# Decode attention on one core: K and V laid out as four heads of two batch rows, 16 partitions each

## The chip, the cores and the metric

The kernel runs on one core of a Trainium2 chip. The metric is the device time of one execution in microseconds (us). Several executions are timed and their median is given.

## The reference

One decode step for four batch rows (B = 4, one token each, width D = 640): layer norm, attention over a cache of Sk = 4096 keys with H = 32 heads of Dh = 128, a residual, layer norm, and a small MLP with the Mish activation. All inputs are bf16.

```
q = (layernorm(x) @ wq).reshape(B, 1, 32, 128).transpose(0, 2, 1, 3)
scores = einsum("bhqd,bhkd->bhqk", q, k_cache) * 128 ** -0.5
o = einsum("bhqk,bhkd->bhqd", softmax(scores), v_cache)
h = x + o.transpose(0, 2, 1, 3).reshape(B, 1, 4096) @ wo
a = layernorm(h) @ w1 + b1            # 640 -> 1728
out = h + (a * tanh(softplus(a))) @ w2
```

The K cache and the V cache hold 4 x 32 x 4096 x 128 values of 2 bytes each, 134.2 MB per cache. Every byte of both is read once.

## The kernel before, in words

The order of all instructions is written out by hand; each engine takes its own in that order.

**Tiling.** One group g is four heads (G = 4) of one batch row: hq, b = divmod(g, 4), 32 groups in all. A head's 4096 keys are spread over 32 partitions (PH = 32), 128 keys in each (R = 128), so K of a group is a tile of 128 partitions with 32 KB each, 4 MB, loaded by one DMA whose 128 rows lie one behind the other in the cache. V has the same layout. There are two K buffers and two V buffers (load_kv, L92 to L101). All these DMAs are issued from the queue of SyncE (SP), in program order: K of g + 2 when group g's products are done with their buffer, then V of g + 1. A DMA that has to wait for its buffer holds up those behind it on SP.

**Scores.** The queries come from q_chunk (L195) and q_broadcast (L209), once per four heads; they are spread to all partitions in qbs. In mul_and_sum VectorE multiplies K in place by the query (L367, two halves of the head dimension for each of two halves of the keys), and TensorE adds groups of columns with the identity matrix as weights, into PSUM (L374, eight matmuls for each product). finish_sum (L386) adds the last eight columns and leaves 128 scores per partition.

**Softmax.** softmax(g) takes the maximum per partition (L397), transposes it with a matmul (L399), takes the maximum per head (L404), spreads it to all partitions (L412, L414), and then ScalarE makes four exponentials per group, one for each head's 32 partitions (L417). Each writes its own column of e2[128 partitions, 128 keys, 4 heads], whose other columns are zero from the start, and its own column of the row sums rs2. Its two halves are put between the products of group g + 1.

**Probabilities times V.** pv_moving (L257) takes four keys per partition at a time: the weights are e2's 16 columns (4 keys x 4 heads), the moving operand is 512 columns of V. Four such matmuls use four disjoint ranges of rows of one PSUM bank p_ps (rows c0 to c0 + 15). pv_copy (L267) copies p_ps to SBUF, and add_blocks (L273) adds up the blocks that belong together with the matrix pick. row_sums (L296), normalise (L307), regroup (L332) and project (L348) follow once per four heads, the last with wo.

**End.** The last K group comes in two DMAs and the last V in four; half of the last V is worked on by pv_stationary (L284), with V as the weights. The weights of the MLP are loaded behind the last V (L502 to L507); w2r_sb is a rest of 64 rows. Then come the layer norm, the first MLP product (L563), the activation (up to L610), the second product (L625) and the output (L649).

Of the kernel before, what the change touches and what calls it, by code (L numbers as in the profile page):

```python
# [8 lines left out]
FP32 = mybir.dt.float32  # L9
# [7 lines left out]
def kernel(  # L17
# [23 lines left out]

    nc = tc.nc
# [4 lines left out]
    N = B * Sq  # L47
    DC = D // 128
    G = 4
    PH = 128 // G  # L50
    R = Sk // PH
    NP = 2
    RP = R // NP
    W = 512 // RP
    HQ = H // G
    NG = HQ * N
# [6 lines left out]
    VP = 4  # L63
    KBUFS = 2
    VBUFS = 2
# [17 lines left out]
    vpool = ctx.enter_context(tc.tile_pool(name="vpool", bufs=VBUFS))  # L83
# [8 lines left out]
    def load_kv(pool, tag, cache, g, parts):  # L92
        hq, b = divmod(g, N)
        t = pool.tile([128, R, Dh], BF16, tag=tag, name=f"{tag}{g}")
        view = cache[b, G * hq : G * (hq + 1)].rearrange("h (p r) d -> (h p) r d", p=PH)

        np_ = parts if g == NG - 1 else 1
        for i in range(np_):
            r0, r1 = i * R // np_, (i + 1) * R // np_
            nc.sync.dma_start(out=t[:, r0:r1, :], in_=view[:, r0:r1, :])  # L100
        return t  # L101

    def load_k(g):
        return load_kv(kpool, "kt", A_k_cache, g, NP)

    def load_v(g):
        return load_kv(vpool, "vt", A_v_cache, g, VP)
# [6 lines left out]
    kts, vts = {}, {}  # L114
    kts[0] = load_k(0)
    kts[1] = load_k(1)
    vts[0] = load_v(0)
# [14 lines left out]
    sel = consts.tile([N, N, G, 128], BF16)  # L132
    nc.vector.memset(sel[:, :, :, :], 0.0)
    e2 = [consts.tile([128, R, G], BF16, name=f"e2_{i}") for i in range(NE2)]
    for t in e2:
        nc.gpsimd.memset(t[:, :, :], 0.0)
    rs2 = consts.tile([128, NG, G], FP32)
    nc.gpsimd.memset(rs2[:, :, :], 0.0)
# [4 lines left out]
    for q in range(G):  # L143
        nc.vector.tensor_copy(
            out=sel[:, :, q, q * PH : (q + 1) * PH],
            in_=ident[0:N, 0:N].unsqueeze(2).to_broadcast([N, N, PH]),
        )
# [42 lines left out]
    q_all = consts.tile([N, H * Dh], BF16)  # L190

    def q_chunk(n):
        q_ps = ps.tile([N, QC], FP32, tag="qq")
        for c in range(DC):
            nc.tensor.matmul(  # L195
                q_ps[:, :],
                lhsT=xT[:, c, :],
                rhs=wq_sb[:, c, n * QC : (n + 1) * QC],
                start=(c == 0),
                stop=(c == DC - 1),  # L200
            )
        nc.scalar.copy(out=q_all[:, n * QC : (n + 1) * QC], in_=q_ps[:, :])  # L202

    def q_broadcast(hq):
        qb_ps = ps.tile([128, N * Dh], FP32, tag="qq")
        for b in range(N):
            for q in range(G):
                h = G * hq + q
                nc.tensor.matmul(  # L209
                    qb_ps[:, b * Dh : (b + 1) * Dh],  # L210
                    lhsT=sel[:, b, q, :],
                    rhs=q_all[:, h * Dh : (h + 1) * Dh],
                    start=(q == 0),
                    stop=(q == G - 1),
                )
        nc.scalar.copy(
            out=qbs[:, hq, :, :], in_=qb_ps[:, :].rearrange("p (b d) -> p b d", d=Dh)
        )

    qbs = consts.tile([128, HQ, N, Dh], BF16)  # L220
# [7 lines left out]
    for hq in Q_AT[-1]:  # L228
        q_chunk(hq)
        q_broadcast(hq)  # L230
# [7 lines left out]
    nc.vector.memset(p_ps[:, :], 0.0)  # L238
    pick = consts.tile([128, J * G], FP32)
    nc.vector.tensor_reduce(  # L240
        out=pick[:, :],
        in_=ident_f[:, :].rearrange("p (t i) -> p i t", t=T)[:, 0 : J * G, :],
# [5 lines left out]
    def ot_of(g):  # L248
        hq, b = divmod(g, N)
        if b == 0:  # L250
            ot[hq] = ps.tile([128, N, G], FP32, tag="ot", name=f"ot{hq}")
        return ot[hq][:, b, :]

    def pv_moving(g, r0, r1):
        for r in range(r0, r1, J):
            c0 = 128 // T * (r // J % T)
            nc.tensor.matmul(  # L257
                p_ps[c0 : c0 + J * G, :],
                lhsT=e2[g % NE2][:, r : r + J, :].rearrange("p j q -> p (j q)"),
                rhs=vts[g][:, r : r + J, :].rearrange("p j d -> p (j d)"),  # L260
                start=(r < J * T),
                stop=(r >= r1 - J * T),
            )

    def pv_copy(g):
        blocks[g] = work.tile([128, J * Dh], FP32, tag="p_sb", bufs=1, name=f"p_sb{g}")
        nc.scalar.copy(out=blocks[g][:, :], in_=p_ps[:, :])  # L267

    def add_blocks(g, stop=True):
        o = ot_of(g)  # L270
        p_sb = blocks.pop(g)
        for j in range(J):
            nc.tensor.matmul(  # L273
                o,
                lhsT=p_sb[:, j * Dh : (j + 1) * Dh],
                rhs=pick[:, j * G : (j + 1) * G],
                start=(j == 0),
                stop=(stop and j == J - 1),
            )
        return o  # L280

    def pv_stationary(g, o, r0):
        for r in range(r0, R):
            nc.tensor.matmul(  # L284
                o,
                lhsT=vts[g][:, r, :],
                rhs=e2[g % NE2][:, r, :],
                start=False,
                stop=(r == R - 1),
            )  # L290
# [3 lines left out]
    def row_sums(hq):  # L294
        l_ps = ps.tile([128, N, G], FP32, tag="small")
        nc.tensor.matmul(  # L296
            l_ps[:, :, :],
            lhsT=ones_f[:, :],
            rhs=rs2[:, hq * N : (hq + 1) * N, :],
            start=True,  # L300
            stop=True,
        )
        rls[hq] = work.tile([128, N, G], FP32, tag="rl", name=f"rl{hq}")
        nc.vector.reciprocal(out=rls[hq][:, :, :], in_=l_ps[:, :, :])  # L304
# [23 lines left out]
    def regroup(hq):  # L328
        o4_ps = ps.tile([128, G, N], FP32, tag="small", name=f"o4_{hq}")
        for q in range(G):  # L330
            for i in range(G):
                nc.tensor.matmul(  # L332
                    o4_ps[q * PH : (q + 1) * PH, i, :],
                    lhsT=ident4[:, i, :],
                    rhs=otn[:, hq, :, q],
                    start=True,
                    stop=True,
                )
# [19 lines left out]
    def mul_and_sum(g, part):  # L358

        hq, b = divmod(g, N)  # L360
# [4 lines left out]
        for k in range(NQ):  # L365
# [4 lines left out]
                in1=qbs[:, hq, b, d0 : d0 + DQ].unsqueeze(1).to_broadcast([128, RP, DQ]),  # L370
# [12 lines left out]
    def finish_sum(g, part):  # L383
        if part == 0:
            s_sbs[g] = work.tile([128, R], FP32, tag="s_sb", name=f"s_sb{g}")
        nc.vector.tensor_reduce(  # L386
            out=s_sbs[g][:, part * RP : (part + 1) * RP],
# [5 lines left out]
    def softmax(g):  # L393

        s_sb = s_sbs.pop(g)
        pm = work.tile([128, 1], FP32, tag="pm", name=f"pm{g}")
        nc.vector.tensor_reduce(out=pm[:, :], in_=s_sb[:, :], axis=AX.X, op=ALU.max)  # L397
        tr_ps = ps.tile([128, 128 + G], FP32, tag="tr", name=f"tr{g}")
# [3 lines left out]
        yield  # L402
        mx = work.tile([1, G], FP32, tag="mx", name=f"mx{g}")
        nc.vector.tensor_reduce(  # L404
            out=mx[:, :],
            in_=tr_ps[0:1, 0:128].rearrange("o (a b) -> o a b", a=G),
# [4 lines left out]
        nb_ps = tr_ps[:, 128 : 128 + G]  # L411
        nc.tensor.matmul(nb_ps, lhsT=nscale[:, :], rhs=mx[:, :], start=True, stop=True)  # L412
        nb = work.tile([128, G], FP32, tag="nbs", name=f"nbs{g}")
        nc.scalar.copy(out=nb[:, :], in_=nb_ps)  # L414
        for q in range(G):
            p0, p1 = q * PH, (q + 1) * PH
            nc.scalar.activation(  # L417
                out=e2[g % NE2][p0:p1, :, q],
                in_=s_sb[p0:p1, :],
                func=ACT.Exp,  # L420
                bias=nb[p0:p1, q : q + 1],
                scale=SCALE,
                accum_out=rs2[p0:p1, g, q : q + 1],
            )
        yield

    for g in range(NG):
        hq, b = divmod(g, N)
        for part in range(NP):
            now = mul_and_sum(g, part)  # L430
            before = None
            next(now)
            if part > 0:
                finish_sum(g, part - 1)
                if g >= 2:
                    add_blocks(g - 2)
                    if b == 1:
                        row_sums(hq - 1)
                        normalise(hq - 1)
                if g in PROJ_AT:  # L440
                    regroup(PROJ_AT[g])
            elif g >= 1:
                finish_sum(g - 1, NP - 1)
                before = softmax(g - 1)
                next(before)
            next(now)
            if before is not None:
                next(before)
# [3 lines left out]
        if 1 <= g < NG - 1:  # L452
            pv_moving(g - 1, 0, R)
            pv_copy(g - 1)
            vts.pop(g - 1)
        if g in PROJ_AT:
            project(PROJ_AT[g])
        if g + 1 < NG:
            vts[g + 1] = load_v(g + 1)
        for n in Q_AT.get(g, ()):  # L460
            q_chunk(n)
            q_broadcast(n)
# [28 lines left out]

    mlp = ctx.enter_context(tc.tile_pool(name="mlp", bufs=1))
# [18 lines left out]


    finish_sum(NG - 1, NP - 1)
    for _ in softmax(NG - 1):
        pass
    pv_moving(NG - 2, 0, R)
    pv_copy(NG - 2)
    row_sums(HQ - 1)
    add_blocks(NG - 2)

    R_LAST = R // 2
    pv_moving(NG - 1, 0, R_LAST)
    pv_copy(NG - 1)
    pv_stationary(NG - 1, add_blocks(NG - 1, stop=False), R_LAST)
# [156 lines left out]
```

## Time and profile before

| | |
|---|---|
| median of 3 runs | 668.12 us (667.93 to 669.77) |
| the profiled execution: its own time | 667.95 us |
| the profiled execution: its span, first to last instruction | 666.0 us |
| moved by DMA | 283.81 MB in 12871 packets, mean 426 GB/s |
| busy: PE (matmul) | 441.5 us, 66% |
| busy: PEld (weight load, beside PE) | 203.6 us, 31% |
| busy: DVE (VectorE) | 352.7 us, 53% |
| busy: ACT (ScalarE) | 114.9 us, 17% |
| mean granted TensorE clock | 0.847 |

How to read it. The span is cut into 40 slices; a digit is the busy share of a slice in tenths, 9 meaning 90% or more. The row DMA is the mean over the 16 DMA engines of the core, and GB/s is what they moved. A group line has the source line, the engine, the operation, output<-inputs by tile names, the shapes, the count, then the total busy time and the mean duration in ns, then the engine's idle time ahead of it and what ended most of that. The issue view lists DMAs by size with the median time from issue to landing. The chain of waits is followed back from the last instruction. Besides the instructions, the trace holds one record for each DMA packet: its start, duration and size.

### The profile page before, as it was taken

The page shows a single profiled execution, that of the slowest core. Times are in us where ns is not written, and L with a number is a line of the kernel's source. Part 1 is how long each engine was busy: PE and PEld are TensorE (multiplying, and loading weights), DVE is VectorE, ACT ScalarE, POOL GpSimd, SP SyncE. Part 2 cuts the span into 40 slices and gives each one's busy share as a digit, 9 for nine tenths or more (in the row PEclk, how much of TensorE's full clock was granted, in tenths as well). Part 3 has the DMA queues.
Part 4 walks back from the last instruction along what each step waited for, and adds up shares of the span by engine and source line. Part 5 has one row for each costly group of instructions (what it writes and reads, how often), then busy time and mean ns, then how long its engine had stood idle before and what let it go on. Part 6 is the DMA issues. An engine that isn't in the chain of part 4 may idle for free.

```text
span 666.0 us, 7149 instructions
## 1 busy us (share of the span) xinstructions
PE 441.5 (66%) x3105; PEld 203.6 (31%) x3105; DVE 352.7 (53%) x306; ACT 114.9 (17%) x352; POOL 2.4 (0%) x13
## 2 busy tenths in 40 slices
PE   0587777897566475377666857756557785667785
PEld 0233233343223232133322323322223332223345
DVE  2486454566645266246654545657444666455742
ACT  0022122122101111011111111111011111011141
POOL 1000000000000000000000000000000000000000
PEclk9998789798778877787777798778789797788985
DMA  9999999999999999999999999999999999999996
GB/s 376 441 434 421 434 440 433 420 436 439 436 419 436 425 434 432 429 437 426 437 433 432 427 435 440 423 432 437 438 424 431 436 438 427 430 433 438 425 418 263
DMA packets 12871, 283.81 MB, mean 426 GB/s; under 512 B 1379, under 2 KB 2087, under 8 KB 4008
## 3 DMA queue, kind: packets, MB, share of 16 engines
q1 hardware_dynamic: 12832, 283.36, 99.0%
q8 instruction: 24, 0.39, 0.2%
q14 instruction: 7, 0.06, 0.0%
q10 hardware_dynamic: 8, 0.01, 0.0%
HBM read 283.35 MB, written 0.01 MB: 425 GB/s over the span
## 4 chain that ended last, share of the span: by engine, by line
DMA 64%; PE 18%; DVE 17%; issue 1%; ACT 0%; SPq 0%; DVEq 0%
DMA kt<-in_A_k_cache_dram 59%; DVE kt L367 14%; PE s L374 14%; DMA w<-in_B_w_dram 3%; DMA vt<-in_A_v_cache_dram 3%; DVE s_sb L386 2%; PE tr L399 1%; PE p_ps L257 1%; PE ot L273 1%; DVE mx L404 0%; PE q_ps L195 0%; PE qb_ps L209 0%; DVE pm L397 0%; PE o L332 0%; ACT q_all L202 0%
## 5 line engine op out<-in xcount | busy, mean ns | idle before, releaser
L374 PE MATMUL s<-kt,ident 128*128 128x512 bf16 x1024 | 295.1, 440 | 193.9 <-DVE kt L367 191.5
L367 DVE TENSOR_TENSOR kt<-kt,qbs 128x4096 bf16<-128x4096 bf16 x128 | 291.5, 2279 | 238.0 <-DMA kt<-in_A_k_cache_dram 238.0
L374 PEld LDWEIGHTS <-ident 128*128 128x128 bf16 x1024 | 109.2, 110 | 337.5 <-issue 167.8
L417 ACT ACTIVATE e<-s_sb,nbs 32x128 bf16<-32x128 f32 x128 | 74.0, 578 | 2.5
L257 PE MATMUL p_ps<-vt,e 128*16 128x512 bf16 x1008 | 64.5, 401 | 0.0
L414 ACT COPY nbs<-tr 128x4 f32<-128x4 f32 x32 | 5.2, 162 | 326.9 <-PE tr L412 326.9
L386 DVE TENSOR_REDUCE s_sb<-s 128x64 f32<-128x512 f32 x64 | 43.5, 680 | 4.0 <-PE s L374 3.9
L267 ACT COPY p_sb<-p_ps 128x512 f32<-128x512 f32 x32 | 18.7, 585 | 154.7 <-PE p_ps L257 154.7
L273 PEld LDWEIGHTS ot<-pick,p_sb 128*128 128x128 f32 x256 | 33.8, 193 | 5.8 <-ACT p_sb L267 1.5
L257 PEld LDWEIGHTS <-e 128*16 128x16 bf16 x1008 | 23.2, 92 | 39.7 <-issue 20.2
L417 ACT ACTIVATION_READ_ACCUMULATOR e<-s_sb,nbs 32x1 f32 x128 | 32.2, 251 | 0.0
L273 PE MATMUL ot<-pick,p_sb 128*128 128x4 f32 x256 | 31.0, 244 | 0.9 <-ACT p_sb L267 0.7
L404 DVE TENSOR_REDUCE mx<-tr 1x4 f32<-1x128 f32 x32 | 8.9, 277 | 23.9 <-PE tr L399 23.9
L195 PE MATMUL q_ps<-wq_sb,xT 128*4 128x512 bf16 x40 | 11.0, 409 | 9.8 <-DMA wq_sb<-in_A_wq_dram 9.8
L399 PE MATMUL tr<-ident_f,pm 128*1 128x128 f32 x64 | 15.2, 329 | 1.2 <-DVE pm L397 1.2
L412 PEld LDWEIGHTS tr<-mx,nscale 1*128 1x128 f32 x64 | 9.4, 182 | 13.8 <-issue 11.4
L304 DVE RECIPROCAL rl<-l_ps 128x16 f32<-128x16 f32 x8 | 2.1, 257 | 21.0 <-PE l_ps L296 21.0
L209 PE MATMUL qb_ps<-q_all,sel 4*128 4x128 bf16 x128 | 9.2, 225 | 5.3 <-ACT q_all L202 5.3
L412 PE MATMUL tr<-mx,nscale 1*128 1x4 f32 x64 | 12.2, 258 | 0.4 <-DVE mx L404 0.4
L209 PEld LDWEIGHTS <-sel 4*128 4x128 bf16 x128 | 8.4, 98 | 9.1 <-issue 9.1
L202 ACT CAST q_all<-q_ps 4x512 bf16<-4x512 f32 x8 | 4.6, 574 | 34.5 <-PE q_ps L195 34.5
L399 PEld LDWEIGHTS tr<-ident_f,pm 128*1 128x1 f32 x64 | 2.8, 80 | 22.9 <-issue 22.9
(85 smaller groups left out, 77.6 us busy)
## 6 DMA issues: line engine op xcount, KB each, us to landing
kt<-in_A_k_cache_dram SPq DMA_DIRECT2D x31, 4096.0 KB, 25.1
vt<-in_A_v_cache_dram SPq DMA_DIRECT2D x31, 4096.0 KB, 33.1
wq_sb<-in_A_wq_dram SPq DMA_DIRECT2D x1, 5120.0 KB
wo_sb<-in_A_wo_dram SPq DMA_DIRECT2D x8, 640.0 KB, 33.9
kt<-in_A_k_cache_dram SPq DMA_DIRECT2D x2, 2048.0 KB
vt<-in_A_v_cache_dram SPq DMA_DIRECT2D x4, 1024.0 KB, 19.0
w<-in_B_w_dram SPq DMA_DIRECT2D x3, 640.0 KB, 17.8
w<-in_B_w_dram SPq DMA_DIRECT2D x1, 1296.0 KB, 25.8
```

Source lines behind the costliest of these rows:

```text
L195: nc.tensor.matmul(q_ps[:, :], lhsT=xT[:, c, :], rhs=wq_sb[:, c, n * QC : (n + 1) * QC], start=(c == 0), stop=(c == DC - 1),)
L209: nc.tensor.matmul(qb_ps[:, b * Dh : (b + 1) * Dh], lhsT=sel[:, b, q, :], rhs=q_all[:, h * Dh : (h + 1) * Dh], start=(q == 0), stop=(q == ...
L257: nc.tensor.matmul(p_ps[c0 : c0 + J * G, :], lhsT=e2[g % NE2][:, r : r + J, :].rearrange("p j q -> p (j q)"), rhs=vts[g][:, r : r + J, :]. ...
L267: nc.scalar.copy(out=blocks[g][:, :], in_=p_ps[:, :])
L273: nc.tensor.matmul(o, lhsT=p_sb[:, j * Dh : (j + 1) * Dh], rhs=pick[:, j * G : (j + 1) * G], start=(j == 0), stop=(stop and j == J - 1),)
L367: nc.vector.tensor_tensor(out=kt[:, :, d0 : d0 + DQ], in0=kt[:, :, d0 : d0 + DQ], in1=qbs[:, hq, b, d0 : d0 + DQ].unsqueeze(1).to_broadcas ...
L374: nc.tensor.matmul(s_ps[:, :, :], lhsT=ident[:, :], rhs=kt[:, :, d : d + W], start=(d == 0), stop=(d == Dh - W),)
L386: nc.vector.tensor_reduce(out=s_sbs[g][:, part * RP : (part + 1) * RP], in_=s_of.pop((g, part))[:, :, :], axis=AX.X, op=ALU.add,)
L399: nc.tensor.matmul(tr_ps[0:1, 0:128], lhsT=pm[:, :], rhs=ident_f[:, :], start=True, stop=True)
L404: nc.vector.tensor_reduce(out=mx[:, :], in_=tr_ps[0:1, 0:128].rearrange("o (a b) -> o a b", a=G), axis=AX.X, op=ALU.max,)
L412: nc.tensor.matmul(nb_ps, lhsT=nscale[:, :], rhs=mx[:, :], start=True, stop=True)
L417: nc.scalar.activation(out=e2[g % NE2][p0:p1, :, q], in_=s_sb[p0:p1, :], func=ACT.Exp, bias=nb[p0:p1, q : q + 1], scale=SCALE, accum_out=r ...
```

## The change

A unit is now four heads of two batch rows (NB = 2, P8 = 8 pairs of row and head), 16 units in all. Each pair has 16 partitions (PH = 16) with 256 keys each (R = 256). The two batch rows alternate by partition: partition 32 q + 2 x + b holds slice x of head q of batch row b. A K tile is half of a unit's keys, 32 KB per partition, with two buffers as before; V of a whole unit is 64 KB per partition in one buffer. As one access pattern can't describe both batch rows, every load is now two DMAs of 64 rows, one to the even and one to the odd partitions (t[b:128:NB]).

One exponential per unit covers all 128 partitions, and a product with a mask of ones and zeros spreads it over eight columns of e2. The row sums take the mask in the same way. The weights of pv_moving have 32 columns. The softmax of a unit stands behind its last sum, no longer between the next group's products, and V's matmuls follow it at once; then V of the next unit is loaded. V of the last two units is loaded in parts. The queries of four heads are kept in a small tile per chunk, and the broadcast for two batch rows takes half the matmuls.

```diff
-    PH = 128 // G
-    R = Sk // PH
+    NB = 2
+    P8 = NB * G
+    PH = 128 // P8
+    R = Sk // PH
+    KT = 2
+    RK = R // KT
...
-    def load_kv(pool, tag, cache, g, parts):
-        hq, b = divmod(g, N)
-        t = pool.tile([128, R, Dh], BF16, tag=tag, name=f"{tag}{g}")
-        view = cache[b, G * hq : G * (hq + 1)].rearrange("h (p r) d -> (h p) r d", p=PH)
-        np_ = parts if g == NG - 1 else 1
-        for i in range(np_):
-            r0, r1 = i * R // np_, (i + 1) * R // np_
-            nc.sync.dma_start(out=t[:, r0:r1, :], in_=view[:, r0:r1, :])
-        return t
+    def load_keys(t, cache, u, keys, dst):
+        hq, bp = divmod(u, N // NB)
+        k0, k1 = keys
+        for b in range(NB):
+            view = cache[NB * bp + b, G * hq : G * (hq + 1)].rearrange("h (p r) d -> (h p) r d", p=PH)
+            nc.sync.dma_start(out=t[b:128:NB, dst : dst + k1 - k0, :], in_=view[:, k0:k1, :])
+
+    def load_k(g):
+        u, k = divmod(g, KT)
+        t = kpool.tile([128, RK, Dh], BF16, tag="kt", name=f"kt{g}")
+        n = NP if g == NG - 1 else 1
+        for i in range(n):
+            r0, r1 = i * RK // n, (i + 1) * RK // n
+            load_keys(t, A_k_cache, u, (k * RK + r0, k * RK + r1), r0)
+        return t
+
+    v_sb = vpool.tile([128, R, Dh], BF16, name="v_sb")
+
+    def load_v(u, r0=0, r1=R):
+        load_keys(v_sb, A_v_cache, u, (r0, r1), r0)
...
+    mask = consts.tile([128, P8], BF16)
+        nc.vector.tensor_reduce(
+            out=mask[:, :].rearrange("p (b q) -> p b q", b=NB),
+            in_=ident[:, :].rearrange("p (q x b) -> p b q x", q=G, b=NB),
+            axis=AX.X,
+            op=ALU.add,
+        )
+    e1 = consts.tile([128, R], BF16)
+    e2 = [consts.tile([128, R, P8], BF16, name=f"e2_{i}") for i in range(NE2)]
...
-                p_ps[c0 : c0 + J * G, :],
-                lhsT=e2[g % NE2][:, r : r + J, :].rearrange("p j q -> p (j q)"),
-                rhs=vts[g][:, r : r + J, :].rearrange("p j d -> p (j d)"),
+                p_ps[c0 : c0 + J * P8, :],
+                lhsT=e2[u % NE2][:, r : r + J, :].rearrange("p j i -> p (j i)"),
+                rhs=v_sb[:, r : r + J, :].rearrange("p j d -> p (j d)"),
...
-        nc.scalar.copy(out=nb[:, :], in_=nb_ps)
-        for q in range(G):
-            p0, p1 = q * PH, (q + 1) * PH
-            nc.scalar.activation(
-                out=e2[g % NE2][p0:p1, :, q],
-                in_=s_sb[p0:p1, :],
-                func=ACT.Exp,
-                bias=nb[p0:p1, q : q + 1],
-                scale=SCALE,
-                accum_out=rs2[p0:p1, g, q : q + 1],
-            )
+        nb8 = work.tile([128, P8], FP32, tag="nb8", name=f"nb8_{u}")
+        nc.vector.tensor_tensor(out=nb8[:, :], in0=nb_ps, in1=mask[:, :], op=ALU.mult)
+        nb = work.tile([128, 1], FP32, tag="nbs", name=f"nbs{u}")
+        nc.vector.tensor_reduce(out=nb[:, :], in_=nb8[:, :], axis=AX.X, op=ALU.add)
+        nc.scalar.activation(
+            out=e1[:, :],
+            in_=s_sb[:, :],
+            func=ACT.Exp,
+            bias=nb[:, :],
+            scale=SCALE,
+            accum_out=rs[:, u : u + 1],
+        )
+        nc.vector.tensor_tensor(
+            out=e2[u % NE2][:, :, :],
+            in0=e1[:, :].unsqueeze(2).to_broadcast([128, R, P8]),
+            in1=mask[:, :].unsqueeze(1).to_broadcast([128, R, P8]),
+            op=ALU.mult,
+        )
...
         kts.pop(g)
         if g + 2 < NG:
             kts[g + 2] = load_k(g + 2)
-        if 1 <= g < NG - 1:
-            pv_moving(g - 1, 0, R)
-            pv_copy(g - 1)
-            vts.pop(g - 1)
+        if k == KT - 1:
+            finish_sum(g, NP - 1)
+            softmax(u)
         if g in PROJ_AT:
             project(PROJ_AT[g])
-        if g + 1 < NG:
-            vts[g + 1] = load_v(g + 1)
+        if k == KT - 1 and u < NU - 2:
+            pv_moving(u, 0, R, R)
+            pv_copy(u)
+            add_blocks(u)
+            if bp == N // NB - 1:
+                row_sums(hq)
+                normalise(hq)
+            if u + 1 < NU - 2:
+                load_v(u + 1)
+            else:
+                load_v(NU - 2, 0, RK)
+        elif k == KT - 1 and u == NU - 2:
+            load_v(u, RK, R)
+            pv_moving(u, 0, RK, R)
+            load_v(NU - 1, 0, RK)
...
+    u = NU - 1
+    pv_moving(u - 1, RK, R, R)
+    pv_copy(u - 1)
+    VQ = RK // 4
+    for r in range(RK, R, VQ):
+        load_v(u, r, r + VQ)
```

## The prediction

> **What bounds the kernel now.** I read the forty slices first, then the stretches, then the chain and the groups, then the DMA issues, and last the single packet records of the trace. The slices of the page:
>
> ```profile
> DMA  9999999999999999999999999999999999999996
> GB/s 376 441 434 421 434 440 433 420 436 439 436 419 436 425 434 432 429 437 426 437 433 432 427 435 440 423 432 437 438 424 431 436 438 427 430 433 438 425 418 263
> ...
> q1 hardware_dynamic: 12832, 283.36, 99.0%
> ```
>
> The 16 DMA engines are busy in every slice but the last. The stretches (from:to, length, then busy time and count of PE, PEld, DVE, ACT, POOL, then clock, DMA share, GB/s) say the same of the middle and show the end:
>
> ```profile
> 300.00:400.00 100.00, 67.54 (x526) 31.14 (x527) 55.22 (x43) 16.01 (x54) 0.00 (x0) 0.81 1.00 430
> 640.00:657.00 17.00, 12.93 (x196) 9.32 (x197) 2.80 (x12) 5.56 (x15) 0.00 (x0) 0.68 1.01 420
> 657.00:663.00 6.00, 3.75 (x107) 3.53 (x105) 1.59 (x7) 1.56 (x3) 0.00 (x0) 0.50 0.51 204
> ```
>
> At 432 GB/s, 283.36 MB take 656 us of a 666.0 us span; DVE has 55 us of work in 100 and PE 68 at a clock of 0.81. The chain and the groups agree: DVE's largest wait is for K, and K's transfers are 59% of the chain.
>
> ```profile
> L374 PE MATMUL s<-kt,ident 128*128 128x512 bf16 x1024 | 295.1, 440 | 193.9 <-DVE kt L367 191.5
> L367 DVE TENSOR_TENSOR kt<-kt,qbs 128x4096 bf16<-128x4096 bf16 x128 | 291.5, 2279 | 238.0 <-DMA kt<-in_A_k_cache_dram 238.0
> ...
> L417 ACT ACTIVATE e<-s_sb,nbs 32x128 bf16<-32x128 f32 x128 | 74.0, 578 | 2.5
> L257 PE MATMUL p_ps<-vt,e 128*16 128x512 bf16 x1008 | 64.5, 401 | 0.0
> ```
>
> A transfer waits some 15 to 23 us behind others before its own 9.7 us (4.19 MB at 432 GB/s) begin, as the issue view's median times to landing show:
>
> ```profile
> kt<-in_A_k_cache_dram SPq DMA_DIRECT2D x31, 4096.0 KB, 25.1
> vt<-in_A_v_cache_dram SPq DMA_DIRECT2D x31, 4096.0 KB, 33.1
> ```
>
> So the kernel is as long as its bytes, plus about 3 us ahead and 3 behind. What counts is what the change does to the rate of the DMA engines, and whether a queue ever runs dry.
>
> **The rate.** The packet records are very even. A 32 KB row takes 1213 ns (7873 of 7936 packets to the nanosecond), a 16 KB row 611, an 8 KB row 309, and the 4-byte packet that closes a DMA on each engine 9. So 16 KB more cost 602 ns, and a packet has some 9 ns of its own. The bytes do not change. V in rows of 64 KB halves the 256 V packets of an engine: 128 x 9 = 1.2 us saved, or nothing if the row is cut into two packets. The closing packets grow, since each K half and each V is now two DMAs: K and V had 33 + 35 = 68 DMAs and will have 66 + 42 = 108, so 40 x 9 = 0.4 us more. Between -0.8 and +0.4; I take -0.5 us, nearest to the row by which a 32 KB packet costs 9 ns less than two of 16 KB.
>
> The 24 packets of the instruction queue cost an engine about 1.4 us each: a gap of some 0.9 us, then a packet some 0.5 us late. Their durations repeat with a period of eight, so I read them as eight engines with three each, 4.2 us, which is the spread with which the engines finish (the 51% DMA share from 657 to 663). The new program has 5334 PE instructions for 5510, and 16 exponentials for 128: perhaps 22 packets for 24, which leaves three on most of those engines. I take 0; below 17 packets it would be 1.4 us less.
>
> **Is each engine as fast when a DMA writes every other partition?** The new DMAs have 64 rows, to partitions 0, 2, 4... or 1, 3, 5.... One DMA of before has 64 rows: w2r_sb, 64 rows of 1280 bytes. Its records show four packets on each of 16 engines, 55 ns each, the same as the 128-row w2s_sb behind it. So 64 rows do use 16 engines, and short rows lose nothing. Long rows on every other partition are nowhere in this trace. If engines do not meet, the cost is 0; if each always shares with another, a packet takes twice 1213 ns, and K and V (268.4 MB, 621 us at 432 GB/s) take 621 us more. Between ends so far apart I take the one that the only 64-row record is nearest to, 0, and keep the other for the range.
>
> [...]
>
> **Does the queue run dry?** A unit is now 16.8 MB or 38.8 us of DMA: K half, K half (9.7 each), V (19.4). Put V(u)'s landing at a. The second K half of u landed at a - 19.4; in before it takes 13.8 us from K's landing (301.4) to the last sum (315.2), softmax of the unit before included, so it is summed by a - 5.6. The softmax now stands alone. From the rows: sum 0.7, maximum 0.3 to 0.6, transpose 0.6, mx 0.3, broadcast 0.4, two small DVE steps 0.4, one exponential of 256 columns 0.6 to 1.2 (L417 has 578 ns at 128) with its 0.25 read, and the mask product of 2048 elements, at L367's rate (4096 in 2279) 1.1 us or at L386's (512 in 680) 2.7. With handovers 6 to 8 us; I take 7. V's 64 matmuls: 32 took 1.9 us (315.13 to 317.03), so 3.8. V(u+1), which needs the one V buffer, is issued at max(a - 5.6 + 7, a) + 3.8 = a + 5.2. Until a + 19.4 the DMA engines have the next two K halves, whose buffers came free earlier. That is 14 us of cover. What waits behind V's issue on SP is the K half after those two, not wanted before a + 38.8. So nothing on the path. Were the cover gone, each unit would lose about 3.8 us of matmuls and 2 us of issue and start, 15 x 5.8 = 87 us.
>
> DVE has per unit 8 x 2.28 + 4 x 0.68 + 4 = 25 us of 38.8, and some 4 us of waits inside the softmax; PE 64 sums at 0.29 us (295.1 / 1024 busy) and 64 V matmuls, about 23. Both stay below, and the DMA hides all of it. ACT drops from 128 exponentials (74.0 + 32.2 us with their reads) to 16. One place could turn: V's matmuls now fill all 32 columns of their group. 401 ns each but 64 in total per matmul says that four groups run together; if the full groups did not, 64 x 0.4 = 26 us a unit would put PE at 45 us and cost some 6 x 15 = 90 us. The groups stay disjoint, so I take 0.
>
> **The end.** In before the chain ends thus:
>
> ```profile
> 627.39 17.00 DMA vt<-in_A_v_cache_dram
> 644.39 0.02 issue
> 644.41 17.39 DMA w<-in_B_w_dram
> 661.80 0.05 issue
> 661.85 1.15 PE y2T L625 x30
> ```
>
> V's last pieces had 17.0 us to land where 9.7 would do, and the weights behind them set the end. After: the last half of V, in four pieces, is issued when the last K half is summed (two products and their sums, 5 to 6 us after its second part lands), its softmax (7) is over and the 32 V matmuls of the unit before (1.9) have read the buffer: 14 to 15 us after that K lands. Two V halves (2 x 9.7 us) are queued ahead of it and still run for some 5 us then. So the weights land as before, up to those -0.5 us. act_t was ready at 660.5, 1.3 us ahead of the last weight, and stays so.
>
> **Sum.** The profiled execution took 667.95 us (span 666.0, 1.9 around it), 0.2 below the median of 668.12. 667.95 - 0.5 + 0 = 667.5. About 0.3% (2 us) is what a measurement of this kernel can tell from no change. Own range of this forecast: 664.5 to 671, from the code packets (-1.4), the rows (-0.8 to +0.4) and an end that loses some of its 5 us of cover.
>
> **Rivals.**
>
> 1. Engines collide, 1200 us. A 64-row DMA gives each engine four rows. [...] From the trace: the engines start K's packets within about 0.4 us of each other. [...] It decides as soon as two engines share over a tenth of their time. For it: the transfers of before are all of 128 rows and all even, so the trace never had to show it. Against: w2r_sb's 55 ns, though 1280 bytes may be too short to show a collision. Chance 0.38.
>
> 2. The queue runs dry through the one V buffer, or PE by its full column groups: 670 to 757. Against it: 14 us of cover, and PE at 23 of 38.8. Chance 0.08.
>
> 3. Faster than 2 us: fewer code packets on the slowest engines and 64 KB rows that save their full 1.2 us, 664. Against: 22 packets leave the slowest engines as they are. Chance 0.06.
>
> 4. The change does less than it says, because each 64 KB row is moved as two packets of 32 KB: 668.3, inside the forecast.
>
> **Numbers.** Forecast with its own range 0.48, of which 0.32 within 0.3%, 0.11 faster, 0.05 slower. Faster 0.11 + 0.06 = 0.17; same 0.32; slower 0.05 + 0.38 + 0.08 = 0.51. Both signs carry weight, so the range runs from 664 to 1230: below lie about 0.06, above about 0.06 of the first rival.
>
> **What would show it.** Right: GB/s near 432 in all slices, 32 KB packets at 1213 ns, V packets at about 2417, DVE's wait for K again the largest. Rival 1: packets at up to twice that, with DMA still 9 in all slices and GB/s near 230. Rival 2: slices of DMA below 9, with SP waiting on p_ps, or PE busy in tenths of 9. The forecast is wrong if 64-row packets are not as even as 128-row ones; nothing else here has a price of that size.

## The result, and the profile after

The changed kernel takes 669.48 us (median of 22 runs, 668.41 to 671.43) for 668.19 us before: ratio 1.002, 95% interval 1.0013 to 1.0026. It is about 1.3 us slower; 667.5 was predicted. The profiled execution's span grew from 666.0 to 667.7 us.

The slices and the main queue of the changed kernel, from its page:

```profile
DMA  9999999999999999999999999999999999999996
GB/s 375 440 442 419 454 410 459 416 433 428 427 450 425 444 413 425 445 418 433 453 415 451 409 455 416 439 426 427 443 432 441 412 451 450 411 419 396 441 387 271
...
q1 hardware_dynamic: 11680, 283.36, 99.0%
```

The DMA engines are as busy as before and, up to 595 us, as fast (432 GB/s from 16 to 595 us in both kernels), with 1152 packets less. Among the last four slices 396 and 387 stand out as low; the last is 271 for 263 before. The stretches (the last three columns are clock, DMA share, GB/s) put the loss into the last 60 us:

```profile
300.00:400.00 100.00, 63.37 (x514) 29.80 (x505) 57.28 (x44) 3.65 (x11) 0.00 (x0) 0.81 1.01 434
400.00:500.00 100.00, 65.01 (x402) 27.75 (x405) 62.07 (x51) 3.14 (x9) 0.00 (x0) 0.84 1.00 431
...
600.00:640.00 40.00, 28.79 (x188) 12.03 (x190) 30.92 (x26) 1.37 (x5) 0.00 (x0) 0.90 0.98 412
640.00:657.00 17.00, 13.38 (x183) 8.76 (x175) 3.02 (x11) 2.66 (x4) 0.00 (x0) 0.60 1.00 395
657.00:663.00 6.00, 3.75 (x98) 3.61 (x96) 1.74 (x7) 2.00 (x4) 0.00 (x0) 0.50 0.87 339
```

From 600 to 640 us 412 GB/s flow, from 640 to 657 us 395, where before had 427 and 420. A finer cut of the same view shows two holes:

```profile
605.00:610.00 5.00, 2.47 (x12) 0.99 (x10) 1.72 (x5) 0.33 (x1) 0.00 (x0) 1.00 0.95 367
610.00:615.00 5.00, 2.35 (x24) 0.95 (x28) 3.87 (x2) 0.27 (x2) 0.00 (x0) 0.62 0.96 374
615.00:640.00 25.00, 20.19 (x140) 8.54 (x136) 20.57 (x17) 0.77 (x3) 0.00 (x0) 0.91 0.99 426
640.00:645.00 5.00, 4.34 (x34) 2.83 (x30) 1.86 (x4) 0.59 (x1) 0.00 (x0) 0.50 0.96 352
```

Before had 446, 426 and 426 GB/s in the three short stretches. The packet records agree. From the first packet of wq to the last of the weights, the DMA engines took 660.2 us before and 661.8 us after. After 570 us of the span, 125 packets are more than 20 ns late, 34.8 us in all or 2.2 us for each of 16 engines; before it was 13 packets and 3.1 us. The engines stood idle for much less, about 9 us between 595 and 652 us or 0.6 us for each, so most of the loss is in packets that take longer while the engines read busy. Elsewhere the packets are as even as before: 65536 bytes in 2418 ns (1781 of 1792), 32768 bytes in 1213 ns (4317 of 4352).

The groups of the page that answer to those shown of before:

```profile
L393 DVE TENSOR_TENSOR kt<-kt,qbs 128x4096 bf16<-128x4096 bf16 x128 | 287.3, 2285 | 99.6 <-DMA kt<-in_A_k_cache_dram 99.6
L400 PE MATMUL s<-kt,ident 128*128 128x512 bf16 x1024 | 268.9, 418 | 119.5 <-DVE kt L393 119.5
...
L276 PE MATMUL p_ps<-v_sb,e 128*32 128x512 bf16 x1008 | 92.3, 545 | 57.4 <-DMA v_sb<-in_A_v_cache_dram 36.6
...
L452 DVE TENSOR_TENSOR e<-e,mask 128x2048 bf16<-128x2048 bf16 x16 | 36.7, 2293 | 11.6 <-ACT e L443 11.6
...
L443 ACT ACTIVATE e<-s_sb,nbs 128x256 bf16<-128x256 f32 x16 | 8.1, 507 | 308.5 <-DVE nbs L442 308.5
```

DVE waits 99.6 us for K in place of 238.0, as it now also makes the mask products (36.7 us) and stands still for parts of the softmax. The V matmuls are as many as before, 1008, and their busy time rose from 64.5 to 92.3 us. The end of the chain of waits:

```profile
610.30 2.31 DVE e L452
612.60 0.04 issue
612.65 3.61 PE p_ps L276 x32
616.25 4.47 PE s L400 x16
...
638.04 3.03 PE p_ps L276 x30
641.07 7.74 DMA v_sb<-in_A_v_cache_dram
648.81 0.02 issue
648.83 14.60 DMA w<-in_B_w_dram
663.43 0.05 issue
663.48 1.16 PE y2T L663 x30
```

The kernel still ends with the weights, but at 663.43 for 661.80. The V piece on this chain lands 7.7 us after the V matmuls release it, where the one on the chain of before took 17.0: hardly anything of the queue is left ahead of it. SP's own timeline shows the K loads that were late as well (start, length, what was issued):

```profile
577.28 1.98 SPq L103 DMA_DIRECT2D v_sb<-in_A_v_cache_dram  x2
596.74 12.71 SPq L103 DMA_DIRECT2D kt<-in_A_k_cache_dram  x6
609.49 30.89 SPq L103 DMA_DIRECT2D v_sb<-in_A_v_cache_dram  x7
```

The half V of unit 14 at 577 is followed by K of g = 30 at 596.74 and by the last K from 606.74 on; the queue's earlier work ran out at about 598 and 609.

### The profile page after: what moved, and what is told of

The parts are those of the page before. It is cut to its first block, busy times and chain, and to the rows that moved or that the text cites. A ratio compares the mean times of both kernels' runs of the same rounds, so it can differ in the third digit from the quotient of the medians.

```text
span 667.7 us, 6506 instructions
## 1 busy us (share of the span) xinstructions
PE 423.4 (63%) x2849; PEld 190.5 (29%) x2849; DVE 389.3 (58%) x330; ACT 34.1 (5%) x80; POOL 1.4 (0%) x10
## 4 chain that ended last, share of the span: by engine, by line
DMA 55%; PE 23%; DVE 19%; issue 1%; SPq 1%; ACT 1%; DVEq 0%; ACTq 0%
DMA kt<-in_A_k_cache_dram 51%; PE s L400 19%; DVE kt L393 15%; PE p_ps L276 3%; DVE s_sb L414 2%; DMA w<-in_B_w_dram 2%; DMA v_sb<-in_A_v_cache_dram 1%; DVE e L452 1%; SPq L103 1%; PE ot L292 0%; ACT e L443 0%; DVE pm L424 0%; PE tr L438 0%; PE tr L426 0%; ACT p_sb L286 0%
## 5 line engine op out<-in xcount | busy, mean ns | idle before, releaser
L393 DVE TENSOR_TENSOR kt<-kt,qbs 128x4096 bf16<-128x4096 bf16 x128 | 287.3, 2285 | 99.6 <-DMA kt<-in_A_k_cache_dram 99.6
L400 PE MATMUL s<-kt,ident 128*128 128x512 bf16 x1024 | 268.9, 418 | 119.5 <-DVE kt L393 119.5
L276 PE MATMUL p_ps<-v_sb,e 128*32 128x512 bf16 x1008 | 92.3, 545 | 57.4 <-DMA v_sb<-in_A_v_cache_dram 36.6
L276 PEld LDWEIGHTS <-e 128*32 128x32 bf16 x1008 | 36.2, 130 | 105.4 <-issue 47.9
L452 DVE TENSOR_TENSOR e<-e,mask 128x2048 bf16<-128x2048 bf16 x16 | 36.7, 2293 | 11.6 <-ACT e L443 11.6
L292 PE MATMUL ot<-pick,p_sb 128*128 128x8 f32 x128 | 17.7, 265 | 11.1 <-ACT p_sb L286 11.1
L443 ACT ACTIVATE e<-s_sb,nbs 128x256 bf16<-128x256 f32 x16 | 8.1, 507 | 308.5 <-DVE nbs L442 308.5
L292 PEld LDWEIGHTS ot<-pick,p_sb 128*128 128x128 f32 x128 | 16.3, 200 | 18.8 <-ACT p_sb L286 18.8
L426 PE MATMUL tr<-ident_f,pm 128*1 128x128 f32 x32 | 6.1, 270 | 20.8 <-DVE pm L424 20.8
L286 ACT COPY p_sb<-p_ps 128x512 f32<-128x512 f32 x16 | 9.4, 586 | 131.2 <-PE p_ps L276 131.2
L438 PE MATMUL tr<-mx,nscale 1*128 1x8 f32 x32 | 6.1, 262 | 5.9 <-DVE mx L430 5.9
```

What stands on the lines that cost most here:

```text
L276: nc.tensor.matmul(p_ps[c0 : c0 + J * P8, :], lhsT=e2[u % NE2][:, r : r + J, :].rearrange("p j i -> p (j i)"), rhs=v_sb[:, r : r + J, :].r ...
L286: nc.scalar.copy(out=blocks[u][:, :], in_=p_ps[:, :])
L292: nc.tensor.matmul(o, lhsT=p_sb[:, j * Dh : (j + 1) * Dh], rhs=pick[:, j * P8 : (j + 1) * P8], start=(j == 0), stop=(stop and j == J - 1),)
L393: nc.vector.tensor_tensor(out=kt[:, :, d0 : d0 + DQ], in0=kt[:, :, d0 : d0 + DQ], in1=qbs[:, g // KT, d0 : d0 + DQ].unsqueeze(1).to_broadc ...
L400: nc.tensor.matmul(s_ps[:, :, :], lhsT=ident[:, :], rhs=kt[:, :, d : d + W], start=(d == 0), stop=(d == Dh - W),)
L426: nc.tensor.matmul(tr_ps[0:1, 0:128], lhsT=pm[:, :], rhs=ident_f[:, :], start=True, stop=True)
```

## The experiments

Times beside each are those of the kernel before in the same job; ratios are against it.

**The loads by themselves.** e2 is the kernel before with nothing changed but its DMAs:

```diff
-            nc.sync.dma_start(out=t[:, r0:r1, :], in_=view[:, r0:r1, :])
+            for b2 in range(2):
+                nc.sync.dma_start(out=t[b2:128:2, r0:r1, :], in_=view[b2:128:2, r0:r1, :])
```

> The kernel before with each K and V DMA cut into two of 64 rows, one to the even and one to the odd partitions, nothing else. Theory A: only the closing packets of 68 more DMAs, 68 x 6 to 9 ns, so +0.4 to +0.6 us, packets of 32 KB at 1213 ns. Rival B: the 64-row form itself explains the +1.3 us of the change or more, with slower packets in the middle of the kernel. Collision rival of the prediction: far slower than 700 us.

Measured: 668.79 us for 668.21, ratio 1.0009 (1.0000 to 1.0018). 7890 of 7936 packets take 1213 ns. From first to last packet it is 660.7 us for 660.2, the +0.5 us of 68 more DMAs. The form of 64 rows on every other partition costs its closing packets; in this run, though, the activation (ready at 661.7, before 660.5) and not the last weight ended the kernel, so the +0.6 us of time are not the closing packets alone.

e3 puts the batch rows on the two halves of the partitions, with mask, sel and the maximum turned to match:

```diff
-            nc.sync.dma_start(out=t[b:128:NB, dst : dst + k1 - k0, :], in_=view[:, k0:k1, :])
+            nc.sync.dma_start(out=t[64 * b : 64 * (b + 1), dst : dst + k1 - k0, :], in_=view[:, k0:k1, :])
```

> The changed kernel with the two batch rows on partitions 0 to 63 and 64 to 127 in place of every other partition; the DMAs are as many and as long. If engines that write the same region of partitions hold each other up, and the alternating layout is what avoids that: K and V at about half rate, packets of 32 KB at about 2420 ns, 1150 to 1290 us. If the layout of the 64 rows does not matter: 669 to 671 us and 1213 ns.

Measured: 1333.21 us, one run. Its page:

```profile
PE 454.0 (34%) x2849; PEld 201.8 (15%) x2849; DVE 391.6 (29%) x330; ACT 34.1 (3%) x80; POOL 1.3 (0%) x10
...
DMA  9999999999999999999999999999999999999998
GB/s 283 220 198 212 218 192 224 197 213 213 198 220 198 231 209 229 217 216 211 220 196 218 201 217 213 200 214 202 218 201 210 218 201 217 206 208 214 217 205 232
```

The DMA engines read as busy as ever and move half: a 32 KB packet takes a median of 2546 ns, a 64 KB packet 5124. A loss as large as the first rival's exists, and every other partition avoids it (1213 and 2418 ns in the changed kernel); whether it comes about as the rival has it, by engines that meet, is not shown here. This run's mean is 213 GB/s, where the changed kernel has 425. Two transfers to every other partition in place of one of 128 rows cost little, with a ratio of 1.0009 in e2.

e4 loads V in rows of 32 KB, by four DMAs for a unit:

```diff
     def load_v(u, r0=0, r1=R):
-        load_keys(v_sb, A_v_cache, u, (r0, r1), r0)
+        for r in range(r0, r1, min(RK, r1 - r0)):
+            n = min(RK, r1 - r0)
+            load_keys(v_sb, A_v_cache, u, (r, r + n), r)
```

> The changed kernel with V of a unit loaded in two halves of the keys, so rows of 32 KB in place of 64 KB, by four DMAs in place of two. If the long row saves what the packet records say (2 x 1213 - 2418 = 8 ns for each of 112 long packets of an engine) and a DMA's closing packet costs 6 to 9 ns: 0.9 us for the rows and about 0.2 us for 28 more DMAs, so 669.5 + 1.1 = 670.6. If the long row saves nothing: 669.7.

Measured: 670.65 us, ratio 1.0034 (1.0021 to 1.0046), 1.2 us over the changed kernel; from first to last packet 662.7 us for 661.8. So the long rows, with the fewer DMAs that they need, did save about a microsecond, as their packets say.

**The end of the queue.** e1 drops the halves: V of unit 14 whole behind unit 13, V of unit 15 behind unit 14's V matmuls.

```diff
-        if k == KT - 1 and u < NU - 2:
+        if k == KT - 1 and u < NU - 1:
...
-            if u + 1 < NU - 2:
+            if u + 1 < NU - 1:
                 load_v(u + 1)
             else:
-                load_v(NU - 2, 0, RK)
-        elif k == KT - 1 and u == NU - 2:
-            load_v(u, RK, R)
-            pv_moving(u, 0, RK, R)
-            load_v(NU - 1, 0, RK)
+                load_v(NU - 1, 0, RK)
+                for r in range(RK, R, RK // 4):
+                    load_v(NU - 1, r, r + RK // 4)
```

> The changed kernel with V of the last two units loaded like every other: V of unit 14 whole as soon as unit 13's V matmuls are done, V of unit 15 right behind unit 14's V matmuls, its last half still in four pieces. Theory A (the loss is the DMA queue running short three times between 598 and 647 us, because the last V loads are halves and are issued late): the dips vanish, the DMA engines move 430 GB/s up to the weights, the time falls by 2 to 3 us from 669.5 to about 667, at or just under the kernel before. Rival B (64-row DMAs, their closing packets or the mask cost a little everywhere): the time stays within 0.5 us of 669.5.

Measured: 675.49 us, ratio 1.0109 (1.0095 to 1.0123). The first half of theory A came true, the second not. The holes are gone (9 late packets after 570 us; 660.0 us from first to last packet, the shortest of all). But the last two K halves now queue behind 8 MB of V. From e1's chain and timeline:

```profile
597.49 24.86 DMA kt<-in_A_k_cache_dram
622.35 0.03 issue
...
651.82 4.71 PE p_ps L276 x48
```

```profile
667.40 0.22 DVE L639 SCALAR_TENSOR_TENSOR act_t<-tb,h1s 128x56 bf16<-128x56 f32 x1
667.67 1.74 PE L654 MATMUL y2T<-act_t,w 128*128 128x4 bf16 x60 [2.10 <-DVE act_t L639]
```

K of g = 30 lands at 622, the activation is ready at 667.6 (before: 660.5), and the 60 matmuls run without a wait for weights. There are two limits at the end: the bytes, and the compute from the last K to the activation.

e7 and e5 try another order. e7 loads unit 14's second V half behind K of g = 30; e5 does so too, and moves unit 14's last V matmuls and the last V load to the end of g = 30 (the lines from `if g == NG - 2` on).

```diff
             kts[g + 2] = load_k(g + 2)
+        if g == NG - 4:
+            load_v(NU - 2, RK, R)
...
-            load_v(u, RK, R)
             pv_moving(u, 0, RK, R)
...
+        if g == NG - 2:
+            pv_moving(NU - 2, RK, R, R)
+            pv_copy(NU - 2)
+            for r in range(RK, R, RK // 4):
+                load_v(NU - 1, r, r + RK // 4)
```

> The changed kernel with one move: the second half of V of unit 14 is loaded behind the K half of g = 30. Theory A: the dip at 609 us vanishes, but the last K half lands 9.7 us later (628 for 621), so the last V half is issued near 646 while the queue ends near 638: a hole of some 8 us and 675 to 678. If the holes did not matter: 669.5.

> The changed kernel with two moves at the end: the second half of V of unit 14 is loaded right behind the K half of g = 30 (in place of behind the last K half), and unit 14's last 32 V matmuls and the load of the last V half stand at the end of g = 30, ahead of the last products and softmax. Theory A (the loss against the kernel before is the short queue at the end): the dips at 609 and 640 us vanish, the small one at 598 stays; DMA ends about 2 us earlier, and the last softmax ends near 644, so the MLP's activation and the last weights come at about the same time, 661 to 662: 667.3 to 668.0, at or under the kernel before. Rival B (the compute chain of the end, longer through the softmax that stands alone, takes over): 669 or more, with the last weights long landed when the activation is ready.

Measured: e7 674.04 us (1.0088; 1.0074 to 1.0101), with a real gap (51 GB/s from 640 to 645 us), as theory A had it, at a slightly smaller price. e5 670.91 us (1.0039; 1.0025 to 1.0053). In e5 the packets take 660.2 us from first to last, the same as before the change, and the activation is ready only at 664.2. Rival B holds for e5.

e6 only moves unit 14's last V matmuls and the last V load, to a place between the halves of the last K tile; e10 only loads 0.66 MB of weights early, into the hole. The lines up to the "..." are e6's, the others e10's.

```diff
             next(now)
+            if g == NG - 1 and part == 0:
+                pv_moving(NU - 2, RK, R, R)
+                pv_copy(NU - 2)
+                for r in range(RK, R, RK // 4):
+                    load_v(NU - 1, r, r + RK // 4)
...
                 load_v(NU - 2, 0, RK)
+                nc.sync.dma_start(
+                    out=w2_first[:, :, :],
+                    in_=B_w2[0 : 128 * CI, :].rearrange("(p i) n -> p i n", i=CI),
+                )
```

> The changed kernel with one move: unit 14's last 32 V matmuls and the load of the last V half stand between the two halves of the last K tile, ahead of the last softmax. Theory A: the dip at 640 us vanishes, the one at 609 stays, 0.9 us less: 668.6. Rival B (those 32 matmuls push the last scores later and the compute chain ends last): 669.5 or more.

> The changed kernel with 0.66 MB of the MLP's second weight matrix (1.5 us of DMA) loaded early, right behind the first half of V of unit 14, where the queue runs short, in place of at the end; the order of all compute stays. Theory A (DMA time is lost in the holes of the short queue): bytes move into the hole at 609 us, from the first packet to the last weight it takes 660.4 us for 661.85; the last weight no longer ends the kernel, the activation does (ready at 661.6 as before), so the time falls by only 0.8 us, to 668.7. If the holes cost nothing: 669.5. If the activation were not next in line: 668.0.

Measured: e6 669.34 us (1.0017; 1.0008 to 1.0026), e10 669.43 us (1.0024; 1.0014 to 1.0034). Both have 660.4 us from first to last packet, as expected, and neither is measurably faster than the changed kernel. The activation stands where the weights stood: ready at 662.5 in e6 and 662.3 in e10. In e10 the hole at 640 stayed (339 GB/s from 640 to 645) and V's last piece landed 1.0 us later. In e6 the hole at 609 stayed (377 and 387 GB/s from 605 to 615), and the moved matmuls put the start of the last sum off from 635.6 to 637.7, as its rival B had it. So the later activation (661.6 in the changed kernel) is in part the price of the edits themselves. Theory A alone, that only the holes cost, does not explain these two runs.

**Both limits at once.** In e6's timeline (start, length, instruction; in brackets what was waited for) the adding up of unit 14's blocks, 1.85 us, stands ahead of the last 48 V matmuls, though the last probabilities are there at 643.55:

```profile
641.26 2.29 DVE L452 TENSOR_TENSOR e<-e,mask 128x2048 bf16<-128x2048 bf16 x1 [0.73 <-ACT e L443]
644.26 1.85 PE L292 MATMUL ot<-pick,p_sb 128*128 128x8 f32 x8
646.04 5.31 PE L276 MATMUL p_ps<-v_sb,e 128*32 128x512 bf16 x48
652.10 1.06 PE L292 MATMUL ot<-pick,p_sb 128*128 128x8 f32 x8 [0.75 <-ACT p_sb L286]
```

e13 is e6 with unit 14's blocks added up ahead of the last softmax and the row sums behind the last V copy; e14 has the blocks and row sums behind the last V matmuls, with the loads of the changed kernel. The diff is e14's; in e13 `add_blocks(u - 1)` stands ahead of `softmax(u)`.

```diff
-    row_sums(HQ - 1)
-    add_blocks(u - 1)
     R_LAST = R - 2 * VQ
     pv_moving(u, 0, R_LAST, R_LAST)
+    add_blocks(u - 1)
     pv_copy(u)
+    row_sums(HQ - 1)
```

> The run e6 (last V half loaded early) with the blocks of unit 14 added up ahead of the last softmax and the row sums behind the last V copy, so that the last unit's V matmuls start as soon as its probabilities are there. Theory C (two limits side by side: the holes in the queue, and a last unit of twice the size whose 48 V matmuls, at the low clock, stand behind its softmax): with both taken away the activation comes about 2 us earlier than in e6 (660.2 for 662.2), the weights end the kernel at the time of the kernel before, 667.8 to 668.4. Theory A alone (only the holes) fell with e6; if something else that these runs do not show holds the end, the time stays at 669.3.

> The changed kernel with the blocks of unit 14 added up, and the row sums taken, behind the last unit's V matmuls in place of ahead of them; the loads stay as they are. Theory C: the holes stay, from the first packet to the last weight it takes 661.8 us as in the changed kernel, the last V pieces are waited for as before: 669.2 to 669.6. If the compute behind the softmax alone set the end: 667.5 to 668.

Measured: e13 668.15 us for 668.04, ratio 0.9999 (0.9990 to 1.0008); e14 669.36 us, 1.0020 (1.0011 to 1.0029). Against the 669.48 of the changed kernel either move alone gives 0.1 us, which is not clear of noise, and the two together 1.3: two limits side by side. (The blocks ahead of the softmax, as in e13, were not run with the loads of the changed kernel.) In e13's timeline the V matmuls follow the probabilities at once, and 640 to 645 us carries 423 GB/s:

```profile
643.83 5.31 PE L276 MATMUL p_ps<-v_sb,e 128*32 128x512 bf16 x48 [3.47 <-DVE e L452]
649.07 0.53 PE L323 MATMUL l_ps<-rs,ones_f 128*128 128x16 f32 x2
649.88 1.06 PE L292 MATMUL ot<-pick,p_sb 128*128 128x8 f32 x8 [0.28 <-ACT p_sb L286]
...
651.99 0.94 PE L303 MATMUL ot<-e,v_sb 128*128 128x8 bf16 x32 [0.25 <-DMA v_sb<-in_A_v_cache_dram]
```

The activation is ready at 661.1 and the last weights are used from 662.40 on. The hole at 609 is still there (377 and 370 GB/s from 605 to 615). e13 equals the kernel before; no version here beats it measurably.

**Holes on purpose.** e8 (the last V was to wait for the buffer of the V ahead of it), e11 and e12 (the load of K of group 18 placed a group later, in the kernel before and in e2) were to show what an empty queue costs with 128 and with 64 rows. The first diff is e8's, to the kernel before.

```diff
-        if g + 1 < NG:
+        if g + 1 < NG - 1:
...
+    finish_sum(NG - 1, NP - 1)
+    for _ in softmax(NG - 1):
+        pass
+    pv_moving(NG - 2, 0, R)
+    pv_copy(NG - 2)
+    vpool.tile([128, R, Dh], BF16, tag="vt", name="skipped")
+    vts[NG - 1] = load_v(NG - 1)
```

The second is e11's, which e12 has in e2:

```diff
+        if g == 17:
+            kpool.tile([128, R, Dh], BF16, tag="kt", name="skipped")
+            kts[18] = load_k(18)
-        if g + 2 < NG:
+        if g + 2 < NG and g != 16:
             kts[g + 2] = load_k(g + 2)
```

> The kernel before, whose last V is made to wait for the buffer of the V ahead of it, so that the queue runs dry once for some 15 us; all transfers have 128 rows. One look at the packets after the hole: if a restart costs only the first packet of each engine, 16 packets of 8 KB are late by 0.5 to 1 us each and all others take 309 ns. Time about 683.

> The kernel before, with K of group 18 loaded one group late, behind K of group 17's products, so that the queue runs dry once in the middle; all transfers have 128 rows. Packets after the hole: only the first of each engine is late (0.5 to 1 us, as at the start of the kernel), all others take 1213 ns. Time 3 to 8 us over 668.2, the length of the hole.

> The same hole, with every K and V transfer as two of 64 rows on every other partition. [...] If 64 rows never collide in this layout: the same packets late, and 0.5 us more for the closing packets alone.

Measured: 668.18 (one run), 667.97 (0.9999; 0.9990 to 1.0008) and 668.78 us (1.0010; 1.0000 to 1.0019). No hole formed, so the question stayed unanswered. The edits hardly put the loads off: in e8 the last V was issued from 627.4 us on, as in the kernel before, and in e11 K of group 18 at 356.4 us, where the kernel before has 353.8. Whether the late packets of the changed kernel's holes (16 KB in up to 2405 ns) are restarts alone, or also engines that hold each other up, is open.

## Why the prediction was wrong, point by point

- **The rate: right, with a smaller saving.** A V row moves as one packet of 2418 ns (2417 predicted), and e4 gives 1.2 us for the rows and their fewer DMAs. An engine saves 112 packets, not 128, as V of the last two units comes in parts, so 1.0 us and not 1.2. Without holes (e1) the new transfers take 660.0 us from first to last packet for 660.2 before, a saving of 0.2 where 0.5 was forecast. The code packets went from 24 to 22, as guessed.
- **64 rows on every other partition: right**, at no cost but closing packets. The first rival, with 0.38, is refuted for this layout by 1213 and 2418 ns; e3 shows that a loss of its size comes with the other way to place the two batch rows. The 1200 us of that rival, on which the upper end of the range rests, no run shows: in the changed kernel 4317 of 4352 packets of 32 KB take 1213 ns, and the other placing, e3, took 1333 us.
- **The middle: right that it costs nothing, with less cover than forecast.** From 16 to 595 us the queue never runs short. The softmax that stands alone takes 5.9 us from its last sum's matmul to the V matmuls (606.7 to 612.6; 7 taken), the mask product 2.3 us (between the 1.1 and 2.7 given). But the 64 V matmuls take 5.2 to 6.6 us for the 3.8 taken (the clock is 0.50 as they start at 534 us). V of unit 13 was issued at 540.5 us and its first packet ran at 549.6: 9 us of cover, not 14.
- **The full column groups: right**, though the busy time of 92.3 us looks otherwise. In e5, 32 of these matmuls took 1.91 us at a granted clock of 1.00 (625 to 630 us), as before (1.90). Behind a softmax they took 3.61 us at 0.50 (612 to 616 us).
- **The end: wrong, and this is the step that failed.** "Two V halves (2 x 9.7 us) are queued ahead of it and still run for some 5 us then" was the cover given to the last V half. It measured none on the DMA engines that finish first. The end of the changed kernel:

```profile
613.42 6.70 DVE L393 TENSOR_TENSOR kt<-kt,qbs 128x4096 bf16<-128x4096 bf16 x3 [0.83 <-DMA kt<-in_A_k_cache_dram]
635.62 0.69 DVE L414 TENSOR_REDUCE s_sb<-s 128x64 f32<-128x512 f32 x1 [1.98 <-PE s L400]
637.97 3.12 PE L276 MATMUL p_ps<-v_sb,e 128*32 128x512 bf16 x32
638.63 3.68 SPq L103 DMA_DIRECT2D v_sb<-in_A_v_cache_dram  x6
```

The last V half was issued from 638.6 us on and its first packet ran at 639.9. Before, the last V pieces were issued from 627.4 on and their first packet ran at 637.1. Two terms behind the 5 us were wrong and nearly cancelled, which is luck. The last packet of the last K half ended at 622.7 and its last sum at 636.3, 13.6 us later for the 5 to 6 taken, because VectorE was still at work on the K half ahead of it, which it could begin only at 613.4, when that had landed. The softmax (7 us) does not stand ahead of unit 14's last V matmuls: they began at 638.0, between its steps. Together 15.9 us for the 14 to 15 taken. What the sum left out is that the DMA engines finish a load some 4 us apart, a spread that the prediction itself had read (here the last K half begins at 608.5 on the first of them, and the K half ahead ends at 613.0 on the last): the last of them moved the V half ahead until 642.1, 3.5 us past the issue, but others stood idle from 639 on.

- **The K loads ahead of it: put at nothing, and wrong.** A V half of 9.7 us in place of 19.4 shortens the cover of the two K loads behind it. K of g = 28 was issued at 556.9 and its first packet ran at 569.0; the last K was issued at 606.7 and its first packet ran at 608.5. Idle time and late packets of one engine come to about 1.4 us from 595 to 616 us (these K loads) and 1.1 us from 637 to 652 us (the last V half); before, to less than 0.1 us in both together. From first to last packet the holes cost 1.8 us (661.8 against 660.0 in e1), less than the sum of the two.
- **"act_t was ready at 660.5, 1.3 us ahead of the last weight, and stays so": wrong too.** The last unit is twice as large; 48 V matmuls, not 16, stand behind its softmax, in 5.1 us at a granted clock of 0.52 (643 to 649 us) for 1.04. The activation came at 661.6 for 660.5. As the weights were late themselves, this did not show in the time of the change; it showed when e6 and e10 each took out one of the holes, where their own edits put the activation off by another 0.9 and 0.7 us, and e13 needed both repairs. How long the changed kernel takes with no holes and its activation at 661.6 was not run.

In sum, the forecast's -0.5 us should have read -0.2 for the bytes and about +1.5 for the end, as the medians differ by 1.3.

## What to carry to other kernels

In a kernel bound by DMA, cover must be recomputed for each transfer near the end, with its own size and on the DMA engine that finishes first: a load cut in half also halves what hides the loads behind it (a V half of 9.7 us in place of 19.4 left the K loads behind it 1.4 us of idle time and late packets on one engine), and a larger work unit puts more compute behind the last byte (48 V matmuls in 5.1 us for 16 in 1.04). Where the last transfer and the last compute come within a microsecond or two of each other, mending one alone may show nothing (0.1 us in e6 and in e14, 1.3 us in e13 with both), so move both before judging either. And 64-row transfers are not one thing: on every other partition they ran at full rate here (32 KB in 1213 ns), on one half of the partitions at half of it (a median of 2546 ns in e3).

## What was not expected of the hardware

- One exponential over 128 partitions x 256 columns, written side by side, took 507 ns, less than the 578 ns of one over 32 x 128 that writes every fourth element.
- The same form of 32 V matmuls took 1.91 us at a granted clock of 1.00 where it stood right behind other matmuls (e5, 626.60 us), and 3.61 us at 0.50 where PE had stood idle for 3.48 us ahead of it (the changed kernel, 612.65 us). What sets the granted clock is not shown here.
- A DMA share of 9 in every slice says nothing of the rate: e3 has it at 213 GB/s.
